# Two unused tiles of 224 bytes that shift where the tiles of an attention and MoE kernel lie in SBUF

## The chip, the cores and the metric

The kernel runs on one core of one Trainium2 chip. The metric is the time of one execution in microseconds on the device; a kernel's time is the median of its runs. Before the change that is 1303.69 us, the median of 3 runs from 1300.96 to 1305.47 us.

## What is computed

First linear attention with a feature map, for 8 batches, 8 heads, 576 positions, head size 64 and 128 features; then RMS norm and a gated feed-forward over the 4608 tokens, model width 512, inner width 1536.

```python
def phi(x):
    proj = np.einsum('bhsd,df->bhsf', x, w_phi)
    proj = proj - np.max(np.abs(proj), axis=-1, keepdims=True)
    return np.concatenate([np.exp(proj), np.exp(-proj)], axis=-1)
q_p, k_p = (phi(q), phi(k))
kv = np.einsum('bhsf,bhsd->bhfd', k_p, v)
z = np.sum(k_p, axis=2)
num = np.einsum('bhsf,bhfd->bhsd', q_p, kv)
den = np.einsum('bhsf,bhf->bhs', q_p, z)[..., None] + 1e-06
...
xn = x / rms * rms_g
g = xn @ w_gate
silu = g * (1.0 / (1.0 + np.exp(-g)))
return (silu * (xn @ w_val) @ w_out).astype(np.float32)
```

## The kernel before

Nearly every matrix product is made three times over: an operand is split into a high part (rounded to fp32r) and a low part (the rest), and high x high, high x low and low x high add up in PSUM (`_split`, L59). A matmul of 128 contraction rows loads 128 columns of weights (the stationary operand) and streams the other operand (the moving one) past them. Both are read from SBUF. Every matmul here loads its weights anew.

The work goes in three stages, one after the other on TensorE:

- **Attention**, the loop at L517 over 32 pairs of heads, as a software pipeline of `front`, `mid`, `back` and `last`. Its fp32r matmuls are the projection (L321 to L323: weights `th`, `tl`, moving `wh`, `wl`, 256 columns) and numerator and denominator (L425: weights `kv`, moving `qh`, `ql`, 288 columns). The sums over keys (L361, 65 columns, and L356, 130 columns) and the transposes (L308, L374) are plain fp32. Between them lie units of `fill` (L484: weights `wf1`, named `fg` and `fv`, moving `xo`, 256 columns), which make the first 3 of the 12 gate and value column blocks. After the last pair, `fill` runs alone (L555).
- **Gate and value**, the loop at L684 over 9 blocks of 512 tokens: `gv` (L626) makes the other 9 column blocks, 2 x 12 matmuls each, with weights `wg`, `wv` or `fg`, `fv` and moving `xb`, 512 columns. `hidden` multiplies and stores to DRAM.
- **Output**, the loop at L796 over 18 groups of 256 tokens. It is a Strassen-Winograd product: `omm` (L807) is called for 7 products, each with 6 values of `kp` times 3 matmuls (L812): weights `a11`, `a12`, `a22`, `s1` to `s4` (tokens), moving `wh{kp}`, `wl{kp}` (the output weights), 256 columns. The pair for `kp` = 0 to 3 comes from the pool `rg` on the right side; that for 4 and 5 comes from `owp4`, `owp5` on the left.

Where a tile lies is set by pools. SBUF has a left side, where pools stack upwards, and a right side, where they stack downwards. Every tile starts at a multiple of 32 bytes within its partition. The left stack begins with five small tiles of the pool `gl` (`eps`, `g`, `one`, `epsd`, `warm`; 4 or 16 bytes, 32 each as laid out), after four constants of 32 bytes each that the framework puts there and a reserved area of 16,384 bytes. Almost all else is a multiple of 256 bytes long, so what the small tiles leave over carries through the whole side. On the right the first pools are `rws` (tile `wr`, L566); they close after the first block (L711), and `rgw` and `rg` are opened there (L712, L713).

The table lists where tiles lie in the built program of before, in bytes within the partition; the last column is the remainder by 128, which is the same for every slice that a matmul reads of the tile.

| tile | role | address | by 64 | by 128 |
|---|---|---|---|---|
| `xb` (two buffers) | moving, L626 | 68,384 and 101,152 | 32 | 32 |
| `xo` (two) | moving, L484 | 60,192 and 68,384 | 32 | 32 |
| `qh`, `ql` | moving, L425 | 143,392 to 171,040 | 32 | 32 |
| `wh4`, `wl4`, `wh5`, `wl5` | moving, L812, left | 82,720 to 124,704 | 32 | 32 |
| `wh0` to `wh3`, `wl0` to `wl3` | moving, L812, right | 163,808 to 213,984 | 32 | 96 |
| projection `wh`, `wl` | moving, L321 to L323 | 125,280 and 126,304 | 32 | 96 |
| `fg`, `fv`, `wg`, `wv`, `a..`, `s..`, `kv`, `th`, `tl` | weights | | 32 | 32 |
| `ek`, `er`, `kt`, `qt`, `rb`, `yq` | weights in fp32 | | 32 | 96 |

Of the kernel before, what the change touches and what calls it, by code (L numbers as in the profile page):

```python
# [8 lines left out]
F32 = mybir.dt.float32  # L9
# [73 lines left out]
def kernel(ctx: ExitStack, tc: tile.TileContext, q, k, v, w_phi,  # L83
# [28 lines left out]

    gl = ctx.enter_context(tc.tile_pool(name="gl", bufs=1))
    rip = ctx.enter_context(tc.tile_pool(name="rip", bufs=2))
    eps = gl.tile([128, 1], F32, name="eps")
    nc.vector.memset(eps, 1e-6)
    g = gl.tile([128, NC], F32, name="g")
# [24 lines left out]
    def fetch(bk, n=T, queue=None):  # L142
        side = len(xips) > 1 and n == TF and (held or bk % 2)
        x = xips[-1 if side else 0].tile([128, NC * (TF if side else T)], F32, name="x")[:, 0:NC * n].rearrange("p (c t) -> p c t", c=NC)
        (queue or nc.sync).dma_start(out=x, in_=xsv[:, :, bk * n:(bk + 1) * n])
        return x

    def prep(bk, x, pool, name):
        ss = xm.tile([128, T], F32, name="ss", bufs=1)
        nc.scalar.activation(ss, x[:, 0], AF.Square)  # L150
        for c in range(1, NC):
            sq = xm.tile([128, T], F32, name="sq", bufs=1)
            nc.scalar.activation(sq, x[:, c], AF.Square)  # L153
            nc.gpsimd.tensor_tensor(ss, ss, sq, ALU.add)  # L154
        sp = pool.tile([128, T], F32, name=name)
        sh = xm.tile([128, T], F32R, name="sq", bufs=1)
        sl = xm.tile([128, T], F32R, name="sl", bufs=1)
        _split(nc, sh, sl, ss, lo_eng=nc.gpsimd)
        nc.tensor.matmul(sp[:, 0:T], ones, sh, start=True, stop=False)
        nc.tensor.matmul(sp[:, 0:T], ones, sl, start=False, stop=True)  # L160
        ri = rip.tile([128, T], F32, name="ri")
        nc.scalar.activation(ri, sp[:, 0:T], AF.Sqrt, scale=1.0 / DM, bias=eps)
        nc.vector.reciprocal(ri, ri)
        for c in range(NC):
            nc.vector.scalar_tensor_tensor(x[:, c], x[:, c], g[:, c:c + 1], ri, ALU.mult, ALU.mult)
        return ri

    def parts(bk, x, ri):
        xhl = xops[bk % len(xops)].tile([128, 2, NC, T], F32R, name="xb")
        for c in range(0, NC, 2):  # L170
            _split(nc, *(a[:, c:c + 2] for a in (xhl[:, 0], xhl[:, 1], x)), lo_eng=nc.gpsimd)
        return xhl[:, 0], xhl[:, 1], ri
# [7 lines left out]
    @contextmanager  # L180
    def late():

        ins = nc.cur_bb.bb.instructions
        n = len(ins)
        with ExitStack() as es:
            for eng in LATE:
                for i in reversed(ins[-300:]):
                    if i.engine == eng and i.name not in waiting:
                        es.enter_context(tc.issue_after(i))
                        break  # L190
            yield
        waiting.update(i.name for i in nc.cur_bb.bb.instructions[n:])
# [419 lines left out]
    def gv(bk, j):  # L612
        if bk == 0 and j + 2 < JN:
            split_gv(j + 2)
        if bk == 0 and j + RW < JN:
            fetch_gv(j + RW)
        xh, xl, _ = xb[bk]
        r = []
        for wi in range(2):
            gp = ps_g.tile([128, 512], F32, name="gp") if wi else ps_h.tile([128, 512], F32, name="gq") if bk else ps_g.tile([128, 512], F32, name="gp")  # L620
            i = 0
            pl = place(wi, j)
            for c in range(NC):
                a, al = pl[0][:, c], pl[1][:, c]
                for w, e in ((a, xh), (a, xl), (al, xh)):
                    nc.tensor.matmul(gp[:, 0:T], w, e[:, c], start=(i == 0), stop=(i == 3 * NC - 1))  # L626
                    i += 1
            r.append(gp[:, 0:T])
        hidden(bk, J1 + j, *r)

    def raw_load(bk, j):
        r = wk.tile([128, 2, T], F32, name="gvr", bufs=1)
        nc.sync.dma_start(out=r, in_=gvv[j][:, :, bk * T:(bk + 1) * T])
        return r

    def gv_raw(bk, j, r):
        nc.vector.tensor_tensor(r, r, xb[bk][2].unsqueeze(1).broadcast_to([128, 2, T]), ALU.mult)
        hidden(bk, j, r[:, 0], r[:, 1])
# [13 lines left out]
    def fetch_o(kp):  # L652
        w, t = (rgw.tile([128, 4, DH], F32, name="wc") for _ in range(2))
        for r, os in ((0, (W11, 3)), (1, (W21, W22))):
            r0 = (2 * kp + r) * 128
            for k, o in enumerate(os):
                nc.sync.dma_start(out=w[:, o], in_=wos[r0:r0 + 128, k * DH:(k + 1) * DH])
        return w, t

    def split_o(kp, pool, wt):  # L660
        w, t = wt
        sub = lambda o, a, b: nc.vector.tensor_tensor(t[:, o], a, b, ALU.subtract)
        sub(0, w[:, 3], w[:, W11])
        sub(2, w[:, W22], w[:, 3])
        sub(1, w[:, W22], t[:, 0])
        sub(3, w[:, W21], t[:, 1])
        wh = pool.tile([128, 7, DH], F32R, name=f"wh{kp}")
        wl = pool.tile([128, 7, DH], F32R, name=f"wl{kp}")
        _split(nc, wh[:, 0:3], wl[:, 0:3], w[:, 0:3])
        _split(nc, wh[:, 3:7], wl[:, 3:7], t)  # L670
        return wh, wl
# [12 lines left out]
    for bk in range(NB):  # L684
        for n, j in enumerate(LAST if bk == NB - 1 else range(JN)):
            gv(bk, j)
            m, k = divmod(n, JN // J1)
            if k == 1:
                with late():
                    gv_raw(bk, m, raw)  # L690
            if k == 2 and (m + 1 < J1 or bk + 1 < NB):
                raw = raw_load(bk, m + 1) if m + 1 < J1 else raw_load(bk + 1, 0)
            if n == 0 and bk + 1 < NB:
                xn = fetch(bk + 1)
            if n == 2 and bk + 1 < NB:
                with late():
                    rin = prep(bk + 1, xn, *((ps_f, "fp") if bk else (ps_g, "gp")))
                first = len(nc.cur_bb.bb.instructions)
                xb[bk + 1] = parts(bk + 1, xn, rin)
                if bk == 0:  # L700
                    waiting.update(i.name for i in nc.cur_bb.bb.instructions[first:])
            if bk and n % 2 == 0 and decs:
                decs.pop(0)()
            if wot and n % 4 == 0:
                with late():
                    wos_ops.append(split_o(len(wos_ops), rg, wot))
                wot = None
            if not decs and not wot and len(wos_ops) < PRE and n % 4 == 1:
                wot = fetch_o(len(wos_ops))
        if bk == 0:  # L710
            raw_ctx.close()  # L711
            rgw = ctx.enter_context(tc.tile_pool(name="rgw", bufs=2, reuse_waits="tile", side="right"))  # L712
            rg = ctx.enter_context(tc.tile_pool(name="rg", bufs=1, reuse_waits="tile", side="right"))  # L713
    g_ctx.close()
# [169 lines left out]
```

## Time and profile before

| | |
|---|---|
| median of the runs | 1303.69 us |
| the profiled execution's own time | 1311.98 us |
| its span, first to last instruction | 1310.2 us |
| mean granted TensorE clock | 0.995 |
| busy share of the span: PE, weight loads, DVE, ACT, POOL | 97%, 91%, 64%, 54%, 47% |
| DMA, mean | 150 GB/s |

A profile shows one execution. A matmul's row gives its start and its duration; matmuls overlap in the array, so a duration is longer than the time that a matmul costs. What a matmul costs in a stream without gaps is the distance from its start to the start of the next, called its pace here. A row of the timeline merges neighbours with one name: the start of the first, the time to the end of the last, and their number. PE's clock at full speed runs 2.4 cycles per ns, and a moving operand passes at one column per cycle, so 512, 288 and 256 columns are 213.3, 120.0 and 106.7 ns.

### The profile page before, as it was taken

The numbers are of one execution on the slowest core, as the hardware profiler recorded it, in microseconds if no ns is written. First come the engines' busy times: TensorE is split into PE (matmuls) and PEld (weight loads), VectorE is DVE, ScalarE is ACT, GpSimd is POOL, SyncE is SP. The second block draws the span as 40 slices with busy tenths as digits, with TensorE's granted clock in tenths as the row PEclk, the third lists the DMA queues.
The fourth block names the chain that finished last, engine by engine and source line by source line (L and its number), as shares of the span: only waits on it lengthen the run. The fifth ranks groups of instructions, "written<-read, shape, count | busy, mean of one in ns | idle before, by whom it ended". The sixth has DMA issues, their size and how long they took to land.

```text
span 1310.2 us, 24148 instructions
## 1 busy us (share of the span) xinstructions
PE 1274.8 (97%) x8886; PEld 1187.7 (91%) x8886; DVE 843.3 (64%) x1228; ACT 705.6 (54%) x1472; POOL 617.8 (47%) x580
## 2 busy tenths in 40 slices
PE   7989999999999898999999999999999999999998
PEld 7989899989999897999888888888888899999998
DVE  7988888878788752411244644644544787887773
ACT  6978787877778874533242342342432444444441
POOL 4666565655555645200323223222211277777773
PEclk9999999999999999999999999999999999999999
DMA  5545666666656347444336435434425555445441
GB/s 164 131 128 147 169 158 178 163 180 167 186 145 194 103 152 222 145 150 143 126 113 201 155 130 189 164 122 149 145 93 168 173 153 154 129 140 159 148 134 49
DMA packets 196164, 197.12 MB, mean 150 GB/s; under 512 B 68880, under 2 KB 151696, under 8 KB 196048
## 3 DMA queue, kind: packets, MB, share of 16 engines
q1 hardware_dynamic: 175168, 172.26, 43.8%
q10 hardware_dynamic: 20880, 23.34, 5.8%
q8 instruction: 70, 1.15, 0.4%
q14 instruction: 46, 0.38, 0.1%
HBM read 126.04 MB, written 69.50 MB: 149 GB/s over the span
## 4 chain that ended last, share of the span: by engine, by line
PE 85%; DMA 5%; DVE 5%; ACT 2%; issue 1%; SPq 1%; POOL 1%; ACTq 0%; POOLq 0%; DVEq 0%
PE gp L626 18%; PE gq L626 15%; PE gd L812 6%; PE gy L812 6%; PE gz L812 6%; PE sm L484 6%; PE acc L361 5%; PE fp L484 5%; PE sm L425 4%; PE fp L812 3%; PE fp L425 2%; PE pp L323 2%; PE sm L374 2%; PE pp L321 2%; PE pp L322 2%; DMA rc<-di 2%
## 5 line engine op out<-in xcount | busy, mean ns | idle before, releaser
L390 POOL TENSOR_TENSOR ql<-eq,qh 128x256 fp32r<-128x256 f32 x256 | 212.0, 860 | 72.3 <-issue 46.4
L609 DVE TENSOR_TENSOR h<-sl,gp 128x512 f32<-128x512 f32 x81 | 55.4, 684 | 166.6 <-PE gp L626 157.7
L626 PE MATMUL gp<-xb,wv 128*128 128x512 f32 x648 | 159.0, 390 | 0.0
L626 PEld LDWEIGHTS gp<-xb,wv 128*128 128x128 f32 x648 | 121.5, 188 | 24.7
L626 PE MATMUL gq<-xb,wg 128*128 128x512 f32 x576 | 138.3, 389 | 0.0
L361 PE MATMUL acc<-vm,ek 128*128 128x65 f32 x1024 | 129.2, 269 | 0.0
L626 PEld LDWEIGHTS gq<-xb,wg 128*128 128x128 f32 x576 | 108.1, 188 | 22.5
L361 PEld LDWEIGHTS acc<-vm,ek 128*128 128x128 f32 x1024 | 125.9, 193 | 0.2 <-ACT ek L348 0.2
L54 POOL TENSOR_TENSOR wa<-raw,wa 128x192 f32<-128x192 f32 (+1 forms) x112 | 64.0, 594 | 128.2 <-DVE wa L52 47.8
L325 DVE TENSOR_REDUCE mx<-pp 128x4 f32<-128x512 f32 (+1 forms) x160 | 100.1, 631 | 37.5 <-PE pp L323 36.0
L386 ACT ACTIVATE qh<-sm 128x512 fp32r<-128x512 f32 (+1 forms) x192 | 97.7, 509 | 0.0
L607 ACT ACTIVATE sl<-gq 128x512 f32<-128x512 f32 x72 | 42.7, 593 | 94.4 <-PE gq L626 92.0
L61 POOL TENSOR_TENSOR xb<-x,xb 128x1024 fp32r<-128x1024 f32 x18 | 47.8, 2678 | 96.9 <-ACT xb L60 96.9
L385 ACT ACTIVATE eq<-sm 128x512 f32<-128x512 f32 x128 | 78.9, 617 | 24.7 <-PE sm L374 22.6
L321 PE MATMUL pp<-wh,th 128*128 128x256 f32 x288 | 87.2, 305 | 3.9 <-DVE yk L328 1.4
L323 PE MATMUL pp<-wh,tl 128*128 128x256 f32 x288 | 83.8, 299 | 0.0
L322 PE MATMUL pp<-wl,th 128*128 128x256 f32 x288 | 81.2, 284 | 0.0
L626 PE MATMUL gp<-xb,fv 128*128 128x512 f32 x324 | 77.8, 389 | 0.0
L348 ACT ACTIVATE ek<-yk 128x512 f32<-128x512 f32 x128 | 75.6, 654 | 4.0 <-DVE yk L328 4.0
L154 POOL TENSOR_TENSOR ss<-ss,sq 128x512 f32<-128x512 f32 x27 | 35.2, 1305 | 85.3 <-ACT sq L153 85.3
L626 PEld LDWEIGHTS gp<-xb,fv 128*128 128x128 f32 x324 | 60.8, 188 | 12.6
L626 PE MATMUL gq<-xb,fg 128*128 128x512 f32 x288 | 69.2, 389 | 0.0
(210 smaller groups left out, 3802.3 us busy)
## 6 DMA issues: line engine op xcount, KB each, us to landing
hs<-h SPq DMA_DIRECT2D x108, 256.0 KB
ht<-hs SPq DMA_DIRECT2D x18, 1536.0 KB
gvr<-gvs SPq DMA_DIRECT2D x27, 512.0 KB
rc<-di SPq DMA_DIRECT2D x32, 288.0 KB
x<-xs ACTq DMA_DIRECT2D x18, 512.0 KB
x<-xs SPq DMA_DIRECT2D x9, 1024.0 KB
gvs<-fo ACTq DMA_DIRECT2D x70, 128.0 KB
kt<-in_k_dram SPq DMA_DIRECT2D x32, 256.0 KB
```

Of the source, the lines that this page charges most:

```text
L321: nc.tensor.matmul(o, th[:, cs], wh, start=True, stop=False)
L322: nc.tensor.matmul(o, th[:, cs], wl, start=False, stop=False)
L323: nc.tensor.matmul(o, tl[:, cs], wh, start=False, stop=True)
L325: nc.vector.tensor_reduce(mx[:, 0:2 * m], pp[:, 0:2 * m], axis=AX.X, op=ALU.max, apply_absolute_value=True)
L361: nc.tensor.matmul(acc[:, sg, h], e[h][:, sg, j], vm[:, h, j], start=False, stop=(h == 1 and j == T0 - 1))
L385: nc.scalar.activation(ei[:, sg], yi, AF.Exp, scale=1.0 - 2.0 * sg)
L386: nc.scalar.activation(hi[:, sg], yi, AF.Exp, scale=1.0 - 2.0 * sg)
L390: nc.gpsimd.tensor_tensor(lo[:, sg, cs], ei[:, sg, cs], hi[:, sg, cs].bitcast(F32), ALU.subtract)
L425: nc.tensor.matmul(o[:, 0:SH], a[:, h, sg], e[:, sg, h, cs], start=(i == 0), stop=(i == 5))
L484: nc.tensor.matmul(fp[:, 0:TF], w, xx[x][:, c], start=(i == 0), stop=(i == 3 * NC - 1))
L626: nc.tensor.matmul(gp[:, 0:T], w, e[:, c], start=(i == 0), stop=(i == 3 * NC - 1))
L812: nc.tensor.matmul(place[n], a[:, kp], w[:, o], start=(first and kp == 0 and i == 0), stop=(kp == KP - 1 and i == 2), skip_group_check=True)
```

## The change

Two tiles of [128, 56] floats, 224 bytes per partition, are allocated and never written or read. One is the first tile of the pool `gl`, so the left side's tiles move up by 224 bytes. The other is the only tile of a new pool on the right, opened after the first block ahead of `rgw` and `rg`, so those move down by 224 bytes.

```diff
     gl = ctx.enter_context(tc.tile_pool(name="gl", bufs=1))
     rip = ctx.enter_context(tc.tile_pool(name="rip", bufs=2))
+    gl.tile([128, 56], F32, name="pad")
     eps = gl.tile([128, 1], F32, name="eps")
...
             raw_ctx.close()
+            pad = ctx.enter_context(tc.tile_pool(name="pad", bufs=1, reuse_waits="tile", side="right"))
+            pad.tile([128, 56], F32, name="rpad")
             rgw = ctx.enter_context(tc.tile_pool(name="rgw", bufs=2, reuse_waits="tile", side="right"))
```

No instruction is added, removed or moved, and none waits for anything else than before: in the built program the 14,696 instructions stand in the same order with the same shapes and the same waits. Only addresses differ. All tiles in the table above now lie at a multiple of 64; by 128 they leave 0, except the projection's `wh` and `wl` and the fp32 weights, which leave 64. `wr` keeps its address (remainder 32 by 64). Some small tiles go the other way, from an even to an odd multiple of 32: `vm1`, `vr0`, `vr2` and one of the two `mx`.

## The prediction

> **What bounds the kernel now.** I read the page first: busy times by engine, then the chain of work that ended last.
>
> ```profile
> span 1310.2 us, 24148 instructions
> PE 1274.8 (97%) x8886; PEld 1187.7 (91%) x8886; DVE 843.3 (64%) x1228; ACT 705.6 (54%) x1472; POOL 617.8 (47%) x580
> PE 85%; DMA 5%; DVE 5%; ACT 2%; issue 1%; SPq 1%; POOL 1%; ACTq 0%; POOLq 0%; DVEq 0%
> ```
>
> PE is the bound; 15% of the chain, some 197 us, belongs to others. Where these lie is seen in the windows, cut by stage (busy us of PE, weight loads, DVE, ACT, POOL; then clock, DMA share, GB/s):
>
> ```profile
> 0.00:520.00 520.00, 489.05 (x3974) 477.44 (x3975) 411.00 (x723) 403.86 (x993) 300.85 (x384) 0.99 0.58 161
> 540.00:620.00 80.00, 80.00 (x643) 78.71 (x642) 17.04 (x22) 32.71 (x75) 3.88 (x3) 1.00 0.46 149
> 640.00:1045.00 405.00, 405.00 (x1796) 335.66 (x1795) 213.21 (x299) 147.13 (x236) 101.51 (x93) 1.00 0.45 148
> 1048.00:1244.00 196.00, 196.00 (x1699) 196.00 (x1698) 153.07 (x135) 82.45 (x108) 149.67 (x68) 1.00 0.48 147
> ```
>
> From 520 us to 1244 us PE never stops, at full clock. There a nanosecond less per matmul is a nanosecond less of time, as long as no other engine fills up: the fullest are DVE at 153 and POOL at 150 of 196 us in the output stage. In attention PE stops for 31 of 520 us and shares the chain with others.
>
> So the question is what one matmul costs in such a stream, and whether its operand's address has a part in that. The timeline on PE gives the pace as the distance of starts. In the gate stage:
>
> ```profile
> 695.05 2.88 PE L626 MATMUL gp<-xb,fv 128*128 128x512 f32 x12
> ...
> 719.53 2.66 PE L626 MATMUL gq<-xb,wg 128*128 128x512 f32 x11
> ```
>
> Between the two stand 8 more rows of 12, so 9 x 12 = 108 matmuls take 24.48 us: 226.7 ns each, where 512 columns at 2.4 per ns are 213.3 ns. That is 544 cycles, 32 above the columns. In the fill units after the last pair:
>
> ```profile
> 566.06 1.60 PE L484 MATMUL sm<-xo,fv 128*128 128x256 f32 x12
> ...
> 570.38 1.60 PE L484 MATMUL sm<-xo,fg 128*128 128x256 f32 x12
> ```
>
> 36 matmuls in 4.32 us: 120.0 ns, 288 cycles, again 32 above the 256 columns. Both moving operands, `xb` and `xo`, lie 32 bytes past a multiple of 128. Now one product of the output stage (first matmul of `kp` = 1, of `kp` = 4, and of the next product):
>
> ```profile
> 1081.05 0.28 PE L812 MATMUL gz<-wh,s1h 128*128 128x256 f32 x1
> ...
> 1082.07 0.28 PE L812 MATMUL gz<-wh,s1h 128*128 128x256 f32 x1
> ...
> 1082.78 0.28 PE L812 MATMUL gd<-wh,s4h 128*128 128x256 f32 x1
> ```
>
> `kp` = 1 to 3, nine matmuls whose moving operand is on the right, 96 past a multiple of 128: 1.02 us, 113.3 ns, 272 cycles, 16 above the columns. `kp` = 4 and 5, six on the left with remainder 32: 0.71 us, 118.3 ns, 284 cycles. The shape is the same, and so is the weights' remainder. The same contrast stands in attention (with the floor of the weights, in the last two rows):
>
> ```profile
> 268.37 0.28 PE L321 MATMUL pp<-wh,th 128*128 128x256 f32 x1
> ...
> 268.71 0.28 PE L322 MATMUL pp<-wl,th 128*128 128x256 f32 x1
> ...
> 272.71 0.29 PE L425 MATMUL sm<-qh,kv1h 128*128 128x288 f32 x1
> ...
> 274.17 0.29 PE L425 MATMUL sm<-qh,kv1l 128*128 128x288 f32 x1
> ...
> 265.80 1.50 PE L361 MATMUL acc<-vm,ek 128*128 128x65 f32 x12
> 267.14 0.60 PE L308 MATMUL sm<-ident,kt 128*128 128x128 f32 x4
> ```
>
> L321 and L322, remainder 96: three in 0.34 us, 113.3 ns, 16 cycles above 256. L425, remainder 32: 11 in 1.46 us, 132.7 ns, 30 cycles above 288. So the surplus doesn't grow with the length (256, 288, 512: 32, 30, 32 cycles); it is a price per matmul, and it goes with the remainder of the moving operand: some 32 cycles at 32, 16 at 96. Nothing of before has a moving fp32r operand at remainder 0, and that is what the change makes of nearly all.
>
> **The change part by part.** Allocating the tiles costs no instruction. What is to be priced is remainder 0.
>
> *The surplus.* I take the simplest reading that gives both prices: the operand comes in units of 128 bytes (32 columns) and a matmul pays for the whole of its last unit. At remainder 32 that unit holds 8 columns of use, so 24 cycles are lost; at 96 it holds 24, and 8 are lost. With a fixed 8 cycles this makes 32 and 16, as measured: one constant, two prices. At remainder 0 nothing is lost, and 8 cycles stay; at 64 it would be 8 + 16 = 24. This is an extrapolation. Its bounds from the rows: no gain at all (the 32 stays), and 0 cycles, which is the columns' own time. In between lies 16, the best price seen.
>
> The Trainium skill (TensorE: Matmul & The Clock Gate, section Back-to-back issue gap) gives a warm matmul N/2.4 + 2.5 ns, 6 cycles above its columns. The trace disagrees as it stands, with 32, 30 and 16; by that rule at remainder 0 L626 would pace at 215.8 ns, and its term below would be 21.1 instead of 19.4 us.
>
> *L626*, 9 blocks x 9 column blocks x 2 x 12 = 1944 matmuls: from 544 to 520 cycles, 10.0 ns each, 19.4 us; nearly all in the stretch where PE never stops. Bounds: 0, and 13.3 ns each or 25.9 us.
>
> *The floor of 256 columns.* L361 moves 65 columns, 27 ns, and yet paces at 1.34 us / 12 = 111.7 ns: there the weight load sets the pace. So 256 columns won't go below about that, though 264 cycles would be 110.0. I take 111.7; bounds 110.0 and the 113.3 seen.
>
> *L484 alone*, after the last pair. The count by tile on this line:
>
> ```profile
> L484 PE MATMUL sm<-xo,fg x312: 274/283/283, 536.0 to 620.5; 128*128 128x256 f32 x156
> L484 PE MATMUL sm<-xo,fv x312: 278/283/283, 536.1 to 621.9; 128*128 128x256 f32 x156
> ```
>
> 624 matmuls x (120.0 - 111.7) = 5.2 us (4.2 to 6.2).
>
> *L812*, 18 x 7 x 18 = 2268 matmuls. Their mean pace is in the chain in order of time, where one kind of row returns after a whole group of 126:
>
> ```profile
> 1060.06 4.16 PE gy L812 x36
> ...
> 1074.62 4.16 PE gy L812 x36
> ```
>
> 14.56 us / 126 = 115.6 ns. To 111.7: 3.9 ns, 8.8 us (5.2 to 12.7). A group then takes 14.07 us; over the window's 196 us that is 7 us, far less than the 43 us by which DVE is free, so PE stays the bound.
>
> *Attention.* L425, 32 x 4 x 6 = 768: 132.7 to 123.3 ns, 7.2 us. The other 672 of L484's 1296: 8.3 ns, 5.6 us. L321 to L323, 32 x 27 = 864: from remainder 96 to 64, by the reading 8 cycles dearer, -2.9 us. The plain fp32 matmuls are at the floor of the weights and stay. Net 9.9 us of PE work; how much reaches the end is bounded by none and all, since waits for the chain below take over:
>
> ```profile
> by line: PE acc L361 13.2%; PE fp L484 10.7%; PE sm L425 8.8%; PE fp L425 5.7%; PE pp L323 4.6%; PE sm L374 4.5%; PE pp L321 4.4%; PE pp L322 4.2%; DMA rc<-di 4.1%; PE sm L308 3.6%; DMA di<-dr 3.6%; issue 2.9%; DVE nd L453 2.3%; DVE mx L325
> ```
>
> I take half, 5.0 us. What is late next there is the round trip of the denominators (`di`, `rc`) and DVE.
>
> *Other engines and DMA* read and write at new addresses too. No row shows what that does to them, and from 520 us on each has slack (POOL 46 us, DVE 43 us in the tightest stage; DMA below half). I put 0; in attention a few us either way.
>
> Sum: 19.4 + 5.2 + 8.8 + 5.0 = 38.4 us. The profiled execution took 1311.98 us (span 1310.2), 0.6% above the median of 1303.69; its paces carry over, so 1303.7 - 38.4 = 1265.3, say 1265.
>
> **The rivals.**
>
> *Half the step.* The unit is 64 bytes: any odd multiple of 32 loses 16 cycles, remainder 0 pays what the best case of before pays, 16 above the columns, and the second 16 at remainder 32 have another cause that goes too. For it: it needs no price outside the rows. Against it: it needs two causes. L626 gains 6.7 ns, 13.0 us; L484 alone 4.2; L812 5.2; attention (768 x 6.0 + 672 x 6.7 ns = 9.1 us) half, 4.5. Together 26.9: 1277.
>
> *No difference.* The 32 cycles belong to an fp32r matmul that reloads its weights, and the cheap cases are cheap for another reason. For it: L626 paces alike with every one of its weight tiles. Against it: the two kinds of moving tile in one product. Time 1304. The Trainium skill's page (SBUF — State Buffer, section Specifications) names cachelines of 16 bytes; by that an odd multiple of 32 is as good as an even one, and this rival would hold. The trace disagrees in so far as 32 and 96, both multiples of 16, differ by 5 ns in L812.
>
> *Slower: same remainder, same bank.* What costs 32 cycles may be that moving operand and weights have the same remainder by 128 and meet in one bank: `xb`, `xo`, `qh` and the left `wh` all lie at 32, as their weights do. The cheap ones lie at 96 against 32. Everything at 0 leaves the dear ones as they are and makes the right side's dear as well: 18 x 7 x 12 = 1512 matmuls x (120.0 - 113.3) = 10.1 us, so 1314. It decides as soon as `kp` = 0 to 3 go from 113 to 120 ns. For it: no row of before has a dear matmul with different remainders. A load is the same for every length, so a fixed price fits this too. Against it: it asks two streams that run at different rates, over tiles at many addresses, to meet equally often every time.
>
> The Trainium skill (SBUF — State Buffer, section Who interferes with whom) says that PE has two independent read ports, for moving operand and weights, and waits for no one, which speaks against this rival; no run here shows it.
>
> That the change doesn't do what it says can be excluded for the tiles of the table; `wr` and some small ones that it misses are no moving operand of a matmul above its floor.
>
> **How the numbers follow.** Forecast 0.42, half the step 0.28, no difference 0.15, slower 0.15. Faster by over 0.3% (about what a measurement of this kernel can tell from no change, 3.9 us) are the first two: 0.70; same 0.15; slower 0.15. The forecast's own range runs from 1246, with 110.0 ns for 256 columns, all of attention's gain and the full bound of L626 (25.9 + 6.2 + 12.7 + 7.2 + 5.6 = 57.6 us), to 1275, with 113.3 ns for 256 columns and nothing in attention (19.4 + 4.2 + 5.2 = 28.8 us). To leave out no more than 2 in 10 the range has to take in no difference: 1246 to 1307.
>
> **What would show it.** Right: L626 from 24.48 to 23.4 us per 108; L484 alone from 4.32 to 4.0 us per 36; the group of 126 from 14.56 to 14.1, with `kp` 1 to 3 and 4 to 5 at the same pace; L425 at 123 ns; L321 to L323 no faster. Half the step: 23.8, 4.08 and 14.3. Wrong: L626 still at 24.48. Then `kp` 1 to 3 tells the rest: 113 is no difference, 120 is the bank.

## The result, and the profile after

The changed kernel takes 1310.6 us (median of 5 runs, 1309.25 to 1313.49) where the kernel before takes 1302.93 (5 runs, 1300.96 to 1305.47): ratio 1.0052, 95% interval 1.0038 to 1.0067, so 5.0 to 8.7 us slower. The profiled execution of after took 1313.49 us. From its page (span, busy times, engines of the chain):

```profile
span 1311.7 us, 24148 instructions
PE 1283.1 (98%) x8886; PEld 1195.6 (91%) x8886; DVE 851.1 (65%) x1228; ACT 704.7 (54%) x1472; POOL 618.4 (47%) x580
PE 87%; DVE 6%; DMA 3%; ACT 2%; SPq 1%; issue 1%; POOL 1%; ACTq 0%; POOLq 0%; DVEq 0%
```

The same 8886 matmuls keep PE busy 8.3 us longer. The windows by stage say where (columns as in the prediction):

```profile
0.00:520.00 520.00, 495.84 (x4020) 483.07 (x4021) 415.34 (x726) 406.63 (x999) 306.60 (x386) 0.99 0.59 165
1048.00:1244.00 196.00, 196.00 (x1636) 196.00 (x1635) 150.58 (x131) 79.29 (x104) 141.68 (x66) 1.00 0.45 140
```

In the same 196 us of the output stage, PE full and at full clock both times, stand 1636 matmuls instead of 1699. DVE and POOL are busy for less of it than before, so no other engine holds PE up: each matmul costs more. The timeline on PE, gate stage (five rows of 12 lie between the two):

```profile
694.72 2.88 PE L627 MATMUL gq<-xb,wg 128*128 128x512 f32 x12
...
711.04 2.88 PE L627 MATMUL gq<-xb,wg 128*128 128x512 f32 x12
```

72 matmuls in 16.32 us, 226.7 ns: as before to the tenth. Fill units alone:

```profile
566.65 1.60 PE L485 MATMUL sm<-xo,fv 128*128 128x256 f32 x12
568.09 1.60 PE L485 MATMUL sm<-xo,fg 128*128 128x256 f32 x12
```

12 in 1.44 us, 120.0 ns, again as before. And one product of the output stage with `kp` = 1, `kp` = 4 and the next product, as the prediction showed it for before:

```profile
1058.83 0.28 PE L815 MATMUL gz<-wh,s1h 128*128 128x256 f32 x1
...
1059.91 0.28 PE L815 MATMUL gz<-wh,s1h 128*128 128x256 f32 x1
...
1060.63 0.28 PE L815 MATMUL gd<-wh,s4h 128*128 128x256 f32 x1
```

`kp` = 1 to 3, the right side: 9 in 1.08 us, 120.0 ns, where it was 113.3. `kp` = 4 and 5, the left side: 6 in 0.72 us, 120.0 ns, where it was 118.3. In the chain a group of 126 was 14.56 us:

```profile
1037.03 4.32 PE gy L815 x36
...
1052.15 4.32 PE gy L815 x36
```

Now it is 15.12 us. 18 groups x 0.56 = 10.1 us; from the first to the last start on its line the output stage took 262.9 us before and takes 272.9. By the starts of all products after the first, before paced `kp` = 0 at 117.7 ns, 1 to 3 at 113.4, 4 at 116.3 and 5 at 119.4 in the mean; after paces all of them at 120.0. So some 8.4 us of the loss lie on the right side and 1.6 on the left. The gate stage, measured so, stays (545.6 and 545.8); it begins before attention ends and takes in the fill units that run alone. The medians differ by 7.7 us. The profiled execution of before had a long attention stage (its gate stage began 8.8 us later than after's), which is why the two profiled times lie only 1.5 us apart.

### The profile page after: what moved, and what is told of

It reads as the page before. It is cut to its first block, busy times and chain, and to the rows that moved or that the text cites. A ratio compares the mean times of both kernels' runs of the same rounds, so it can differ in the third digit from the quotient of the medians.

```text
span 1311.7 us, 24148 instructions
## 1 busy us (share of the span) xinstructions
PE 1283.1 (98%) x8886; PEld 1195.6 (91%) x8886; DVE 851.1 (65%) x1228; ACT 704.7 (54%) x1472; POOL 618.4 (47%) x580
## 4 chain that ended last, share of the span: by engine, by line
PE 87%; DVE 6%; DMA 3%; ACT 2%; SPq 1%; issue 1%; POOL 1%; ACTq 0%; POOLq 0%; DVEq 0%
PE gp L627 18%; PE gq L627 15%; PE gd L815 6%; PE gz L815 6%; PE gy L815 6%; PE acc L362 6%; PE sm L485 6%; PE fp L485 5%; PE sm L426 4%; PE fp L815 3%; PE fp L426 2%; PE pp L324 2%; PE pp L322 2%; PE sm L375 2%; PE pp L323 2%; PE sm L309 2%
## 5 line engine op out<-in xcount | busy, mean ns | idle before, releaser
L391 POOL TENSOR_TENSOR ql<-eq,qh 128x256 fp32r<-128x256 f32 x256 | 215.4, 872 | 64.3 <-issue 38.9
```

Of the source, the lines that this page charges most:

```text
L391: nc.gpsimd.tensor_tensor(lo[:, sg, cs], ei[:, sg, cs], hi[:, sg, cs].bitcast(F32), ALU.subtract)
```

## The experiments

In all that follows, the *displacement* is the moving operand's address less the weights' address, modulo 256 bytes. Before: 192 for the right side of the output, 0 for its left side, for `xb` and for `xo`, 64 for the projection. After: 0 for the right side too, all others unchanged. That is everything the change does to the matmuls' addresses, if only the difference counts. Theory: it does. Rival: the moving operand's own address counts.

**m1_offsets**: the price by itself.

```diff
+# columns, moving operand's bytes past a multiple of 128, the weights' bytes past it
+GROUPS = [(512, m, 0) for m in (0, 0, 16, 32, 48, 64, 80, 96, 112, 128)]
+GROUPS += [(512, 32, 32), (512, 64, 32), (512, 96, 32), (512, 0, 64)]
+GROUPS += [(256, m, 0) for m in (0, 16, 32, 48, 64, 80, 96, 112)]
+GROUPS += [(256, 96, 32), (288, 0, 0), (288, 32, 0), (288, 64, 0)]
...
+            nc.tensor.matmul(a[:, 0:n], wt[:, w0:w0 + 128], mv[:, m0:m0 + n], start=(j == 0), stop=(j == 23))
```

> Only streams of 24 fp32r matmuls, each with its own weight load, on tiles cut from q; the rest of the computation is left out. Each stream has its own place of the moving operand and of the weights by 128 bytes. Meeting (the price goes by the difference of the two places): with the weights at 0, 512 columns pace at 226.7 ns for the moving operand at 0 and 128, and at 220 ns or less at 64; at (32, 32) 226.7 again, at (96, 32) and (0, 64) 220 or less. Own address (the price goes by the moving operand's place alone, dear in the lower half of 128 bytes): (0, 64) and (32, 32) at 226.7, 64 and 96 at 220 whatever the weights. 256 columns: 120.0 where 512 are dear, 113.3 or the weights' floor of 111.7 where they are cheap. Neither says what 16, 48, 80 and 112 do.

Its timeline; each row is a stream of 24, here (moving, weights) at (0, 0), then (16, 0), at (32, 0), then (48, 0), and at (32, 32), (64, 32), (96, 32):

```profile
17.27 5.60 PE L38 MATMUL gpa<-mv,wt 128*128 128x512 f32 x24
22.71 5.72 PE L38 MATMUL gpb<-mv,wt 128*128 128x512 f32 x24
28.27 5.77 PE L38 MATMUL gpa<-mv,wt 128*128 128x512 f32 x24
33.87 5.76 PE L38 MATMUL gpb<-mv,wt 128*128 128x512 f32 x24
...
67.25 5.62 PE L38 MATMUL gpb<-mv,wt 128*128 128x512 f32 x24
72.72 5.77 PE L38 MATMUL gpa<-mv,wt 128*128 128x512 f32 x24
78.32 5.67 PE L38 MATMUL gpb<-mv,wt 128*128 128x512 f32 x24
```

From start to start: (0, 0) 5.44 us, 226.7 ns a matmul; (32, 0) 5.60, 233.3; (32, 32) 5.47, of which the first few matmuls still settle and the last twelve pace at 226.7; (64, 32) 5.60, 233.3. Likewise (64, 0) and (96, 32) both pace at 228.8 ns in their last twelve. A move of both operands by 32 changes nothing, a move of one does: the own address is out, and for 512 columns the displacement 0 that the gate stage has is the cheap one. The 220 ns or less that both readings expected of some places appeared nowhere.

**e1_right64**, the whole change with the right side's displacement put back to 192:

```diff
-            pad.tile([128, 56], F32, name="rpad")
+            pad.tile([128, 72], F32, name="rpad")
```

> The changed kernel with 288 instead of 224 unused bytes on the right: the right side's output weights lie at 64 by 128, everything else as in the changed kernel, at 0. Meeting and own address alike: L815 on the right back from 120.0 to 113.3 ns, a group of 126 matmuls from 15.12 to 14.6 us, 1512 x 6.7 ns = 10 us less than the changed kernel, about 1301. If the changed kernel is slower for another reason than the right side, it stays at 1310.

1303.15 us, ratio 0.9993 (0.9972 to 1.0015). The chain:

```profile
1064.38 4.16 PE gy L815 x36
...
1078.93 4.16 PE gy L815 x36
```

14.55 us a group, the output stage 263.1 us: the loss is gone, with every other tile where the change puts it. So the loss is the right side's displacement, and the rest of the change is worth nothing that these runs can tell (between 0.28% faster and 0.15% slower).

**e4_left64**, before with 64 bytes ahead of the left side's tiles alone: the right side's displacement becomes 128, while all tiles stay at odd multiples of 32.

```diff
+    gl.tile([128, 16], F32, name="pad")
```

> The kernel before with one unused tile of 64 bytes ahead on the left: left tiles at 96 by 128, weights too, the right side's at 96 as before; all stay odd multiples of 32. Meeting: moving operand and weights are level everywhere, L627 stays at 226.7, L813 goes to 120.0 on the right: 1313, as slow as the changed kernel. Own address: all moving operands at 96, so L627 at 220 (-13.0 us), L485 and L813 at 113.3: 1277.

1311.13 us, ratio 1.0065 (1.0044 to 1.0086). A group takes 14.96 us (118.7 ns), the output stage 270.0 us. The left tiles at 96 gain nothing.

**e2_right_level** and **e3_right_alone** move the right side alone, to 128 and to 224:

```diff
+            pad = ctx.enter_context(tc.tile_pool(name="pad", bufs=1, reuse_waits="tile", side="right"))
+            pad.tile([128, 16], F32, name="rpad")
```

(56 instead of 16 floats in e3_right_alone.)

> The kernel before with 64 unused bytes on the right alone: the right side's output weights go from 96 to 32 by 128, level with the tokens' 32; no tile becomes an even multiple of 32. Displacement: L814 on the right at 120.0 ns, a group of 126 at 15.12 us, 10.1 us slower, 1313, with attention and gate as before. Parity of 32 bytes: nothing gets slower, 1303.

> The change's right-hand tile alone: the right side's output weights lie at 0 by 128, all else as before at 32, a displacement of -32 bytes. Displacement: neither level nor the 192 of before; the first streams had 116.8 ns at +32 and 119.9 at +96, so 117 to 120 ns on the right and 5 to 10 us slower than before, 1308 to 1313. Parity of 32 bytes: the even place of the moving operand makes it faster than before, below 1300.

1310.86 us, ratio 1.005 (1.0025 to 1.0075), and 1310.69, ratio 1.0038 (1.0025 to 1.0052). Right side 118.7 and 118.1 ns, output stage 270.0 and 269.5 us. The right half of the change alone costs about what the whole does, and so does any other place that the right side's displacement has been moved to so far: 192 was a good one. At displacement 128, in e2_right_level as in e4_left64, the pace is 118.7 ns and not the 120.0 that was expected of operands level by 128.

**w64_apart**, before with `apart` pads of 64 bytes around the pools of the moving tiles, so that no moving operand has its weights' remainder by 128:

```diff
+    def apart(es, name):
+        es.enter_context(tc.tile_pool(name=name, bufs=1, reuse_waits="tile")).tile([128, 16], F32, name="pad")
...
+    apart(g_ctx, "p4")
+    xo1 = own("xo1")
```

> The kernel before with pairs of unused 64-byte tiles around the pools of xo, of qh and ql, of both xb, and of the output weights on the left: these moving operands lie at 96 by 128 while all weights stay at 32. Meeting and own address alike: L627's successor at 220 ns (-13.0 us), fill units at 113.3 (-4.2 alone after the last pair), output group at 14.3 us (-5.2), numerators at 126.7 with half of attention's gain (-4.5): 1277. If 32 cycles are the price of 512 columns in any place, only the fill units, the output and the numerators gain: 1290.

A miss: 1309.8 us, ratio 1.0049 (1.0028 to 1.0071). The gate stage grew from 545.6 to 554.0 us. Its timeline, against the same weight tiles, once with one of the two `xb` buffers and once with the other:

```profile
698.35 2.96 PE L638 MATMUL gp<-xb,wv 128*128 128x512 f32 x12
...
709.55 2.96 PE L638 MATMUL gp<-xb,wv 128*128 128x512 f32 x12
...
743.38 2.91 PE L638 MATMUL gp<-xb,wv 128*128 128x512 f32 x12
...
754.36 2.91 PE L638 MATMUL gp<-xb,wv 128*128 128x512 f32 x12
```

11.20 us for 48, 233.3 ns, at displacement 192, and 10.98 us for 48, 228.8 ns, at 64, instead of 226.7 at 0. So the theory of a bank by 128, in which the same remainder is the dear one, fails as well: for 512 columns it is the cheapest.

**s512, s256, s288**: the streams of m1_offsets over all displacements in steps of 16 (s512 and s256 up to 1008); the line is that of s256.

```diff
+GROUPS = [(256, 0, 0)] + [(256, m, 0) for m in range(0, 1024, 16)]
```

> Only streams of 24 fp32r matmuls of 512 columns with a weight load each, the moving operand displaced by 0, 16, ..., 1008 bytes against the weights; the rest of the computation is left out. Displacement (the price goes by the distance between the two operands, not by either address): one curve, 226.7 ns at 0, up to 234 elsewhere, that repeats after 256 or 512 bytes. If the two reads can be placed so that they never meet, some displacement is below 220 ns; if every load costs 32 cycles of the moving stream anyway, none is below 226.7.

> The same with 256 columns. Displacement: 120.0 ns at 0, 113.3 at 112, 117.8 at 64, as in the first streams, and 113.3 at 192 (the place of the right side's output weights before) in place of 120.0; the same period as with 512 columns. If the pace depended on more than the displacement, 192 would not give 113.3.

> Only streams of 24 fp32r matmuls of 288 columns with a weight load each, displacement 0 to 240 bytes in steps of 16; the rest of the computation is left out. Displacement: 131.5 ns at 0 and 132 to 133 at 64 and 32 as in the first streams; the lowest place between 126.7 (16 cycles above the columns) and 131.

ns a matmul, worked out from the last 12 distances between starts in each stream of 24:

```
displacement   0   16    32    48    64    80    96   112   128   144   160   176   192   208   224   240
512 columns 226.7 231.7 233.3 233.3 228.9 231.2 233.3 231.1 232.5 233.3 234.2 233.3 233.3 234.5 233.3 226.7
288 columns 131.7 131.7 133.3 133.1 131.7 131.1 131.7 134.3 133.3 130.0 133.3 131.8 133.3 133.3 133.3 132.0
256 columns 120.0 118.5 116.7 118.3 117.8 120.0 120.0 113.3 118.8 118.5 117.1 119.3 113.3 119.7 118.6 116.7
```

Up to 1008 the 512 and 256 columns repeat with a period of 256 bytes within 0.1 ns. Each length has its own curve. Every stream here is entered from the displacement 16 below its own; s_entry, further down, shows that another entry can give another pace. Before's gate stage stood at the best place of this table for 512 columns and its right side at the best for 256; the change moved these 1512 matmuls to one of the dearest.

**o192 and w192**: before with all output at 192, and with the filler and the projection there as well (`apart` takes the number of floats).

```diff
+    apart(ctx, "p8", 48)
     owps = [left("owp4")]
+    apart(ctx, "p9", 16)
```

> The kernel before with 192 unused bytes ahead of each of the two left pools of output weights and 64 behind: both now at a displacement of 192 against the tokens, like the right side's. Displacement: L821 at 113.3 ns on both sides, a group of 126 from 14.56 to 14.28 us, 18 x 0.28 = 5.0 us less, 1298.7. If the first product's matmuls (kp 0), dear on entering the right side, were dear for another reason, they stay at 353 ns for three.

> As the one before, and xo at 192 against fg and fv, the projection's weights at 192 (from 64) against th and tl; xb and its weights stay level, where the curve for 512 columns has its lowest place. Displacement: output -5.0 us; fill units alone at 113.3 ns, 624 x 6.7 ns = -4.2 us; in attention 672 x 6.7 + 864 x 4.5 ns = 8.4 us of PE work, of which half reaches the end, -4.2: together 13.4 us less, 1290, and faster than both kernels. If attention's waits take it all, 1294.

Both miss: 1308.23 us, ratio 1.0025 (1.0007 to 1.0043), and 1303.88, ratio 0.9992 (0.9976 to 1.0009). The chain of o192:

```profile
1068.89 4.24 PE gy L819 x36
...
1083.73 4.24 PE gy L819 x36
```

14.84 us a group, 117.8 ns, on both sides, at the displacement that gave 113.3 in before; the output stage is 267.9 us, 5.0 longer. In w192 it is 267.8. There the filler is at 117.8 ns too, so the stretch in which it runs alone goes from 86.0 to 84.5 us; as the median is level with before's, the rest of what the output lost came back in attention or lies in the spread of the runs; no run takes it apart. The first output product of before, ahead of any left matmul, and `kp` = 1 and 4 of its second product show the same two paces at one place:

```profile
1043.21 0.28 PE L812 MATMUL fp<-wh,a11h 128*128 128x256 f32 x1
...
1044.62 0.28 PE L812 MATMUL fp<-wh,a11h 128*128 128x256 f32 x1
...
1045.69 0.28 PE L812 MATMUL gy<-wh,a12h 128*128 128x256 f32 x1
...
1046.71 0.28 PE L812 MATMUL gy<-wh,a12h 128*128 128x256 f32 x1
```

12 right matmuls in 1.41 us, 117.5 ns; six left ones at displacement 0 later, 9 in 1.02 us, 113.3. The next three kernels ask whether a stream has two steady paces.

**s_entry**: streams of 256 columns at 192 and at 112, each entered from every other displacement `d`.

```diff
+GROUPS = [(256, 0, 0)] + [(256, x, 0) for d in range(0, 256, 16) for x in (d, 192, d, 112)]
```

> Streams of 24 matmuls of 256 columns with one weight load each, and nothing of the reference: a stream at displacement d, then one at 192, then d again, then one at 112, for every d from 0 to 240 in steps of 16. The displacement is the moving operand's address less the weights', modulo 256 bytes. Theory: the displacement alone does not set the pace; two steady paces exist at 192, 113.3 ns (before's right side output) and 117.8 ns (the same displacement in the kernel with all output at 192), and what ran before settles which of them is kept. So the streams at 192 come out in two groups, 113.3 and 117 to 118 ns, by d; 113.3 at least for d of 0 and 176 (0 stands before the right side's matmuls in before, 176 in the sweep). At 112 either two groups too, or 113.3 after every d. Rival: the displacement alone sets the pace and the kernel with all output at 192 is slower for another reason (its new tile places): then 192 gives 113.3 ns after every d, and 112 as well.

The timeline, at 192 after 0 (and the next stream's start), and at 192 after 16:

```profile
17.60 2.90 PE L35 MATMUL gpb<-mv,wt 128*128 128x256 f32 x24
20.34 3.02 PE L35 MATMUL gpa<-mv,wt 128*128 128x256 f32 x24
...
28.83 2.99 PE L35 MATMUL gpb<-mv,wt 128*128 128x256 f32 x24
31.66 3.01 PE L35 MATMUL gpa<-mv,wt 128*128 128x256 f32 x24
```

2.74 us and 2.83 us for 24 matmuls of the same addresses. By the last 12 distances of each stream: at 192, 117.8 ns after `d` = 16, 144 and 160, and 113.3 after the other 13; at 112, 113.3 after all 16 (after 208 the settling reaches into the last 12, 114.4). Entering takes up to some 14 matmuls. So two paces at 192 are shown, and what ran before settles which is kept; each entry ran once, those from 112 and 192 twice. The streams at `d` show that 192 is not alone in this. At 144, after 112 and then after 192 (the row behind each is the next stream's start):

```profile
115.32 3.01 PE L35 MATMUL gpa<-mv,wt 128*128 128x256 f32 x24
118.17 2.99 PE L35 MATMUL gpb<-mv,wt 128*128 128x256 f32 x24
120.99 2.88 PE L35 MATMUL gpa<-mv,wt 128*128 128x256 f32 x24
123.71 2.92 PE L35 MATMUL gpb<-mv,wt 128*128 128x256 f32 x24
```

2.85 us, 118.8 ns, and 2.72 us, 113.3 ns: after 192, displacement 144 is as cheap as the best places of the table, which has 118.5 for it.

**o112 and w112**: the displacement that had one pace, in the kernel: all output at 112; then filler and projection too.

```diff
-        wh = pool.tile([128, 7, DH], F32R, name=f"wh{kp}")
-        wl = pool.tile([128, 7, DH], F32R, name=f"wl{kp}")
+        a = 44 if kp < PRE else 28
+        x = pool.tile([128, 14 * DH + 64], F32R, name=f"wh{kp}")[:, a:a + 14 * DH]
+        wh, wl = (x[:, i:i + 7 * DH].rearrange("p (o n) -> p o n", o=7) for i in (0, 7 * DH))
```

> The kernel before with all the output weights' tiles moved so that the moving operand lies 112 bytes past the stationary one, modulo 256. If 112 has only the pace of the sweep, 113.3 ns: the 1512 right matmuls go 114.5 to 113.3 and the 756 left ones 117.8 to 113.3, 1.8 + 3.4 = 5.2 us, about 1298.5. If 112 also has a second, slower pace that is kept, 117 to 118 ns as at 192: 1512 x 3.3 = 5.0 us more, about 1309.

> The same with the filler's operand and the projection's weights at 112 as well. With 113.3 ns throughout: 1296 filler matmuls go 120.0 to 113.3, 8.7 us, and 864 of the projection 117.8 to 113.3, 3.9 us at most, beside the 5.2 us of the output: about 1286 if TensorE stays the bound of that stage. With 117 to 118 ns kept: 2.9 us from the filler less 5 us of the output, about 1306.

1299.08 us, ratio 0.9955 (0.9938 to 0.9971), and 1292.61, ratio 0.9915 (0.9896 to 0.9934): the fastest of all. o112 came out as expected of a single pace; w112 gained 11.9 us of the 18 expected. The chain of o112, and the filler in w112:

```profile
1063.32 4.08 PE gy L813 x36
...
1077.60 4.08 PE gy L813 x36
```

```profile
545.23 1.52 PE L484 MATMUL sm<-xo,fv 128*128 128x256 f32 x12
546.59 1.52 PE L484 MATMUL sm<-xo,fg 128*128 128x256 f32 x12
```

14.28 us a group, 113.3 ns on both sides; the output stage 258.1 us, 4.8 less than before, against 5.4 us in the medians. The filler alone goes to 1.36 us per 12, 113.3 ns, and the stretch in which it runs alone from 86.0 to 82.1 us. The terms within attention gave less than expected: the projection's pace stayed at 118 to 119 ns in the median. Its matmuls come mostly in runs of six or fewer between others, which is shorter than the settling at 112 in most entries of s_entry; that this is the reason was not tested.

## Why the prediction was wrong, step by step

- *The bound* held: PE is full from the gate stage on, at full clock, and its pace is time. That is why most of the 10.0 us that the output stage lost show in the medians (7.7).
- *The price goes with the moving operand's remainder*: wrong, and with it *The surplus*, "the operand comes in units of 128 bytes (32 columns) and a matmul pays for the whole of its last unit". At remainder 0 the gate stage's matmuls still paid 32 cycles, and m1_offsets gives the same pace for (0, 0) and (32, 32). This is the step that failed; in its place the runs show a price that goes with the displacement, and at some places with what ran before. The rows of before had only one remainder of the weights, 32, so own remainder and displacement could not be told apart in them; two prices were fitted with two constants. The trace of before did hold rows that would have tested the reading. `kp` = 0 has remainder 96 as `kp` = 1 to 3 have, and paced at 117.7 ns. The projection has remainder 96 too; three of its matmuls at 113.3 ns were shown, but over that trace the distances between neighbouring starts of the projection (532, leaving out those over 150 ns) are 118 ns in the median. s256 has 117.8 for its displacement, 64.
- The terms that rest on it (19.4, 5.2, 8.8 and 5.0 us) are all zero or less. The paces of L626 (226.7 ns) and of L484 alone (120.0) stayed. So did those in attention, in the median of both traces 118 ns for the projection, 120 for the filler and 133 for the numerators. The output term came out as -10.1 instead of 8.8.
- *The floor of 256 columns* was neither reached nor refuted: no run paced 256 columns below 113.3 ns.
- *Other engines and DMA at 0* held within the interval of e1_right64 (0.9972 to 1.0015).
- *Same remainder, same bank* had the sign and the place (`kp` = 1 to 3 from 113 to 120 ns). That its 10.1 us came out to the tenth is partly luck: it priced 1512 matmuls at 6.7 ns, but `kp` = 0 started from 117.7, so the right side lost some 8.4 us, and the left side, which the rival expected to stay, lost the other 1.6. Left and right alternate, and in before the left side's pace still rose from `kp` = 4 to 5 (116.3 and 119.4 ns) after the cheaper right side. Its picture is not right: the same remainder is dear for 256 columns and cheapest for 512, and e3_right_alone, with remainders 0 and 32, loses nearly as much (118.1 ns). What I held against it, that two streams at different rates would have to meet equally often every time, is what s_entry answers: the streams settle into a steady pace, sometimes one of two. The rule of the Trainium skill that was weighed there (SBUF — State Buffer, section Who interferes with whom: two independent read ports, and PE waits for no one) is not borne out for these two reads: in m1_offsets, where only the copies and stores of the results run beside the streams, their displacement alone makes 226.7 or 233.3 ns of one matmul.
- *Half the step* and *No difference* fail by the group of 126, 15.12 us.

Open: the loss by the trace is 10.1 us and by the medians 5.0 to 8.7; what the rest of the change might give back is inside the interval of e1_right64. Which resource the two reads share, why each length has its own curve, and why some entries lead to the dearer pace was not tried.

## What to carry to other kernels

Where TensorE is full and reloads its weights for each matmul, take the pace from start to start for each kind of tile, and list it beside the distance between the two operands' addresses before moving any tile. A pad is then a knob that can lose as well as win: try the whole range of it on a bare stream of the same length, enter it from what runs before it, and prefer a place with one pace. A price law read off rows that vary one operand only needs a row in which the other one moves.

## What the runs showed of the hardware

- The pace of an fp32r matmul with a new weight load depends on the displacement modulo 256 bytes of moving operand and weights: 226.7 to 234.5 ns for 512 columns (s512), 130.0 to 134.3 for 288 (s288), 113.3 to 120.0 for 256 (s256). Moving both operands by the same 32 bytes changed nothing (m1_offsets).
- One displacement can have two steady paces with 256 columns: 113.3 and 117.8 ns at 192, 113.3 and 118 to 119 at 144, by what ran before (s_entry). The slower one at 192 was kept for a whole stage of 2268 matmuls (o192).
- Alignment to 64 or 128 bytes by itself was worth nothing here (e1_right64, ratio 0.9972 to 1.0015).
